# A retention recurrence followed by a Mish feed-forward block: list-scheduled order, early chunks with states carried by TensorE, late DMA transposes

## The chip, the cores and the metric

One core of one Trainium2 chip. The metric is device time in microseconds (us), median of several executions. "Span" is the length of one profiled execution; in the profiled runs of this case the reported time is 1.7 to 1.9 us longer than the span. TensorE is PE in the profile, VectorE DVE, ScalarE ACT, GpSimd POOL, SyncE SP; PEld are TensorE's weight loads.

## The reference

```python
# q, k, v: (B, H, S, D) = (4, 8, 768, 64), float32; w_in: (512, 2048), w_out: (2048, 512)
gamma = 1.0 - 2.0 ** (-5.0 - arange(H))
for t in range(S):                                   # one state of 64x64 per batch and head
    state = gamma * state + outer(k[:, :, t], v[:, :, t])
    y[:, :, t] = q[:, :, t] @ state / sqrt(D)
x = y.transpose(0, 2, 1, 3).reshape(3072, 512)
h = x @ w_in
out = (h * tanh(softplus(h))) @ w_out                # Mish, then the second product
```

## The kernel before

The 3072 tokens are cut into 12 groups of 256 (two chunks of 128; three groups make one batch). In a group, four "units" (pairs of heads) do the recurrence in chunked form. A unit transposes k and q on TensorE, computes the masked products of q and k, updates the state, and forms y from two products that add up in PSUM. Then `f1` is the first product with Mish, in 8 slices per group, and `f2` is the second product.

```python
def step_t(u):                       # transposes on TensorE, three copies on VectorE
    for c in range(CG):
        nc.tensor.transpose(tp[:, 1, c], k16[:, c, hs(hp)], ident)
    for c in range(CG):
        nc.tensor.transpose(tp[:, 0, c], q16[:, c, hs(hp)], ident)
    nc.vector.tensor_copy(kt, tp[:, 1])
    nc.vector.tensor_copy(qp[0:64, :, 0], tp[0:64, 0])      # q padded with zeros, per head
    nc.vector.tensor_copy(qp[64:128, :, 1], tp[64:128, 0])
# step_s: s_ps = kt x qp; am = s_ps * msk; u_ps = k16 x v16; new state = old * gamma**C + u_ps
def step_y(u):
    # ...
        nc.tensor.matmul(y_ps[:, c], v16[:, c, hs(hp)], am[:, c], start=True, stop=st is None)
        if st is not None:                                   # 2 x 128 columns of padded q
            nc.tensor.matmul(y_ps[:, c], st, qp[:, c], start=False, stop=True)
    # ... two half copies to xt on ScalarE

# order of the loads
load(0)
for j in range(NW):
    load_win(j)
load(1); load(2)
# ... cast(0)
for j in range(NW):
    load_wout(j)
load(3)
# order of the work: fixed by hand
for i in range(NG + 2):
    if i + 2 < NG:
        cast(i + 2)                  # q, k, v of two groups ahead, on GpSimd
    if i == 0:
        for j in range(NW):
            cast_wout(j)             # on GpSimd too, behind cast(2)
    # ... load(i + 3)
    for a in range(NSL):             # 8 slices
        # ... the next attention step or steps
        if i < NG:
            f1(i, a)
        if 0 <= i - 2:
            f2(i - 2, a)             # the second product lags by two groups
```

## Time and profile before

| | before |
|---|---|
| median time | 249.91 us (4 runs, 249.44 to 253.05) |
| profiled span | 250.4 us |
| TensorE busy | 220.4 us (88%), 1,696 matmuls |
| TensorE idle before 54 us | 25.2 us |
| last matmul to the end | 3.7 us |

The first view is the second part of the page of the kernel before: busy tenths in 40 equal slices of 6.3 us. PEclk is the clock granted to TensorE.

```profile
PE   0263199949999999999999999999999999999993
...
PEclk9999999998999999999999999999999999999999
DMA  8999999999912914916808609519210111011122
```

TensorE is full from the tenth slice on and mostly empty in the first five. The next view gives busy time in four stretches of the kernel before. Idle time is the length minus the first "busy" figure; the last three columns are granted clock, mean busy share of the DMA engines (as it is counted here it can read above 1), and GB/s.

```profile
core 0: us, PE busy (x) PEld busy (x) DVE busy (x) ACT busy (x) POOL busy (x), PEclk, DMA share, GB/s
0.00:22.00 22.00, 8.04 (x44) 4.85 (x44) 11.29 (x34) 4.94 (x10) 3.54 (x8) 1.00 1.05 285
22.00:54.00 32.00, 20.81 (x189) 17.27 (x189) 19.70 (x46) 13.80 (x29) 25.31 (x12) 1.00 1.16 272
54.00:246.70 192.70, 191.58 (x1463) 135.37 (x1463) 84.88 (x230) 76.53 (x157) 56.25 (x26) 0.99 0.43 97
246.70:250.40 3.70, 0.00 (x0) 0.00 (x0) 0.64 (x1) 0.00 (x0) 0.00 (x0) 0.92 0.19 71
```

From 54 us on there is 1.1 us of idle time in 193, so nearly only less TensorE work can shorten that stretch. (From 55 to 59 us the granted clock is 0.57, which costs 1.7 us more, right after a wait of 3.7 us.) In front of it 14.0 + 11.2 us are idle. What those wait for is in the chain of waits (the work that ended last, followed back), in order of time:

```profile
12.25 11.25 DMA raw_q<-in_q_dram
23.63 2.32 POOL q_276 L119
26.37 1.99 POOL k_277 L121
...
47.47 5.45 DMA raw_k<-in_k_dram
53.08 1.91 POOL k_504 L121
55.48 1.71 PE h_ps L228 x8
```

The q of group 1 (raw_q) sits behind 4 MB of w_in and lands at 23.5 us; its casts on GpSimd follow. The k of group 3 (raw_k, cast as k_504) lands at 52.9 us. In between TensorE has only attention of groups 0 to 2 and first products of groups 0 and 1: the fixed order puts the transposes of group 3's first unit before the last first products of group 1, and has no second product before the first product of group 2. So TensorE waits 3.7 us for k_504, until 55.0 us.

The groups of instructions show the rates:

```profile
L228 PE MATMUL h_ps<-xt,win_87 128*128 128x256 f16 x768 | 101.9, 277 | 0.0
L241 PE MATMUL o_ps<-wout_88,gt 128*128 128x512 f16 x384 | 95.9, 379 | 0.0
L209 PE MATMUL y_ps<-qpad_91,tstate 128*128 128x256 f16 x28 | 7.4, 285 | 0.0
```

After the first bar stand the busy time of the group and the mean duration of one in ns, after the second the idle time before them. Matmuls overlap, so the pace is not that mean: in the timeline eight h_ps start within 0.87 us (109 ns each).

### The profile page before, as it was taken

How to read it: one execution, taken by the hardware profiler on the slowest of the kernel's cores; microseconds unless marked ns; L12 is line 12 of the kernel's file. 1: busy time of each engine (PE TensorE's matmuls, PEld its weight loads, DVE VectorE, ACT ScalarE, POOL GpSimd, SP SyncE). 2: the span in 40 equal slices, each digit the busy share in tenths (PEclk: the TensorE clock that was granted, in tenths of full speed). 3: DMA queues.
4: the chain of work that ended last, by engine and by line, in shares of the span. 5: the costliest groups of instructions: out<-in, count | busy, mean ns of one | idle time of the engine just before them, and what ended most of it. 6: DMA issues, size and time to landing. Idle time of an engine off the chain costs nothing.

```text
span 250.4 us, 4251 instructions
## 1 busy us (share of the span) xinstructions
PE 220.4 (88%) x1696; PEld 157.5 (63%) x1696; DVE 116.5 (47%) x309; ACT 95.3 (38%) x195; POOL 85.1 (34%) x45
## 2 busy tenths in 40 slices
PE   0263199949999999999999999999999999999993
PEld 0141178827777777777777777777777777766441
DVE  1478567624455454535545553444655444101221
ACT  0324037624434445344444434444443444533000
POOL 3102997679940450460640822703600000000000
PEclk9999999998999999999999999999999999999999
DMA  8999999999912914916808609519210111011122
GB/s 162 297 387 263 218 287 387 256 207 227 181 42 66 225 46 106 195 40 149 190 0 176 162 3 229 106 46 228 66 42 0 45 45 41 3 42 45 44 81 84
DMA packets 82868, 33.91 MB, mean 135 GB/s; under 512 B 75552, under 2 KB 75680, under 8 KB 82848
## 3 DMA queue, kind: packets, MB, share of 16 engines
q1 hardware_dynamic: 82560, 33.56, 56.9%
q8 instruction: 13, 0.21, 0.4%
q10 hardware_dynamic: 288, 0.08, 0.1%
q14 instruction: 7, 0.06, 0.1%
HBM read 27.34 MB, written 6.29 MB: 134 GB/s over the span
## 4 chain that ended last, share of the span: by engine, by line
PE 77%; SPq 9%; DMA 7%; POOL 4%; issue 2%; DVE 0%; POOLq 0%
PE o_ps L241 33%; PE h_ps L228 29%; SPq L103 8%; DMA raw_q<-in_q_dram 4%; PE s_ps L174 3%; PE y_ps L205 3%; PE y_ps L209 3%; DMA raw_k<-in_k_dram 2%; PE tp L157 2%; PE tp L159 2%; PE u_ps L182 1%; SPq L130 1%; POOL q_276 L119 1%; POOL k_277 L121 1%; POOL k_504 L121 1%
## 5 line engine op out<-in xcount | busy, mean ns | idle before, releaser
L228 PE MATMUL h_ps<-xt,win_87 128*128 128x256 f16 x768 | 101.9, 277 | 0.0
L241 PE MATMUL o_ps<-wout_88,gt 128*128 128x512 f16 x384 | 95.9, 379 | 0.0
L232 ACT ACTIVATE gt<-h_ps 128x512 f16<-128x512 f32 x96 | 57.3, 597 | 96.0 <-PE h_ps L228 95.7
L228 PEld LDWEIGHTS <-win_87 128*128 128x128 f16 x768 | 72.7, 99 | 9.6
L241 PEld LDWEIGHTS <-gt 128*128 128x128 f16 x384 | 37.6, 98 | 28.2
L212 ACT CAST xt<-y_ps 64x256 f16<-64x256 f32 x96 | 35.1, 365 | 31.1 <-PE y_ps L209 30.5
L176 DVE TENSOR_TENSOR am<-s_ps,msk 128x512 f16<-128x512 f32 x48 | 33.0, 687 | 26.9 <-PE s_ps L174 26.8
L162 DVE COPY kt<-tp 128x256 f16<-128x256 f16 x48 | 14.0, 291 | 52.3 <-PE tp L159 52.3
L246 DVE COPY osb<-o_ps 128x512 f32<-128x512 f32 x24 | 16.6, 691 | 42.6 <-PE o_ps L241 42.6
L191 DVE SCALAR_TENSOR_TENSOR tstate<-tstate,tab,u_ps 128x128 f16<-128x128 f16 x64 | 21.9, 342 | 1.1
L174 PEld LDWEIGHTS <-kt 128*128 128x128 f16 x96 | 9.9, 105 | 8.7
L209 PEld LDWEIGHTS <-tstate 128*128 128x128 f16 x80 | 8.1, 101 | 4.1 <-DVE tstate L189 0.3
L157 PE MATMUL tp<-idtri,k_142 128*128 128x128 f16 x8 | 1.6, 308 | 10.1 <-DVE k_142 L121 9.2
L157 PE MATMUL tp<-idtri,k_277 128*128 128x128 f16 x8 | 1.3, 260 | 8.6 <-POOL k_277 L121 7.8
L142 POOL CAST wout_88<-wst 128x2048 f16<-128x2048 f32 x4 | 7.6, 1893 | 3.4 <-DMA wst<-in_moe_w_out_dram 3.2
L119 POOL TENSOR_TENSOR q_276<-raw_q,tab 128x1024 f16<-128x1024 f32 x1 | 2.8, 2777 | 16.1 <-DMA raw_q<-in_q_dram 16.1
L157 PEld LDWEIGHTS <-k_142 128*128 128x128 f16 x8 | 0.8, 126 | 10.6 <-DVE k_142 L121 9.2
L209 PE MATMUL y_ps<-qpad_91,tstate 128*128 128x256 f16 x28 | 7.4, 285 | 0.0
L209 PE MATMUL y_ps<-qpad_92,tstate 128*128 128x256 f16 x28 | 7.1, 278 | 0.0
L157 PEld LDWEIGHTS <-k_277 128*128 128x128 f16 x8 | 0.7, 110 | 9.5 <-POOL k_277 L121 8.2
L174 PE MATMUL s_ps<-qpad_91,kt 128*128 128x256 f16 x32 | 6.6, 291 | 0.0
L174 PE MATMUL s_ps<-qpad_92,kt 128*128 128x256 f16 x32 | 6.6, 291 | 0.0
(147 smaller groups left out, 226.9 us busy)
## 6 DMA issues: line engine op xcount, KB each, us to landing
raw_q<-in_q_dram SPq DMA_DIRECT2D x24, 256.0 KB, 5.0
raw_k<-in_k_dram SPq DMA_DIRECT2D x24, 256.0 KB, 5.1
raw_v<-in_v_dram SPq DMA_DIRECT2D x24, 256.0 KB, 5.0
out_dram<-osb SPq DMA_DIRECT2D x24, 256.0 KB, 2.0
wst<-in_moe_w_in_dram SPq DMA_DIRECT2D x4, 1024.0 KB, 9.2
wst<-in_moe_w_out_dram SPq DMA_DIRECT2D x4, 1024.0 KB, 10.4
idtri<-rn_identtri ACTq DMA_DIRECT2D x1, 64.0 KB, 3.1
tab<-rn_tab ACTq DMA_DIRECT2D x1, 10.0 KB, 1.9
```

Of the source, the lines that this page charges most:

```text
L103: nc.sync.dma_start(t[:, c], src[b, :, s0:s0 + C].rearrange("h p d -> p h d"))
L157: nc.tensor.transpose(tp[:, 1, c], k16[:, c, hs(hp)], ident)
L162: nc.vector.tensor_copy(kt, tp[:, 1])
L174: nc.tensor.matmul(s_ps[:, c], kt[:, c], qp[:, c], start=True, stop=True)
L176: nc.vector.tensor_tensor(am, s_ps, msk[:, hs(hp)].unsqueeze(1).broadcast_to((P, CG, 2, C)), op=ALU.mult)
L191: nc.vector.scalar_tensor_tensor(tn, states[-1], tab[:, 2 * H + hp:2 * H + hp + 1], u_ps[:, c], op0=ALU.mult, op1=ALU.add)
L209: nc.tensor.matmul(y_ps[:, c], st, qp[:, c], start=False, stop=True)
L212: nc.scalar.copy(xt[o:o + 64, hp, g * GT:(g + 1) * GT].rearrange("p (c i) -> p c i", i=C), y_ps[o:o + 64, :, hh])
L228: nc.tensor.matmul(h_ps[:, j], win16[:, bp, fb * P:(fb + 1) * P], xt[:, bp, i * GT:(i + 1) * GT], start=(bp == 0), stop=(bp == NBP - 1))
L232: nc.scalar.activation(gts[i][:, 2 * a:2 * a + 2], h_ps, AF.Mish, scale=inv_boost3)
L241: nc.tensor.matmul(o_ps, gts[i][:, fb, t * P:(t + 1) * P], wout16[:, fb], start=(fb == 0), stop=(fb == NFB - 1))
L246: nc.vector.tensor_copy(osb, o_ps)
```

## The change

The intent: keep TensorE fed from about 20 us on, and give it less to do.

1. **Order by a list scheduler.** The kernel describes 916 timed tasks with priorities, dependencies and buffer slots. `Plan.run` simulates five engines, each of which starts the ready task of highest priority, and the instructions are emitted in the simulated order. Attention goes before first products, these before second products; the lag of two groups is gone.
2. **Early groups (0 and 1).** Group 0 is loaded, cast and computed in single chunks, loads are ordered groups 0, 1, w_in, w_out, then 2, 3, 4, and the old state enters the new one through an identity matmul.
3. **Late groups (5 to 11).** k and q are transposed by DMA. In groups 2 to 11 the state is kept block-diagonal, so its product streams 128 columns of unpadded q.
4. y fills full 128 partitions with zero-padded v, so ScalarE evacuates it in one copy.

```diff
+class Plan:
+    LAT = {"PE": 0.25, "DVE": 0.1, "ACT": 0.1, "POOL": 0.12, "DMA": 2.0}
+    # ... tasks, ready heaps by (prio, id), slots counted per buffer tag
+    plan = Plan(
+        {"raw_q": 3, "raw_k": 3, "raw_v": 3, "grp": 3, "wst": 4, "am": 2, "xt": 3,
+         "gt": 5, "out": 2, "tp": 1, "s": 1, "u": 1, "y": 1, "h": 2, "o0": 1, "o1": 1})
+    sts = [[cpool.tile([P, P], FP16, name=f"st{h}_{i}") for i in range(3)] for h in range(HP)]
     # ...
+    def dma_transpose(g):                      # g >= DT = 5
+            nc.sync.dma_start_transpose(
+                casts[g]["kt"].rearrange("p c x j -> p (c x) j"),
+                casts[g]["k16"].rearrange("p c h d -> p (c h d)"))
     # ... the same for q, then VectorE pads q
-            nc.tensor.matmul(y_ps[:, c], v16[:, c, hs(hp)], am[:, c], ...)
-            if st is not None:
-                nc.tensor.matmul(y_ps[:, c], st, qp[:, c], start=False, stop=True)
+                for hh in range(2):
+                    nc.tensor.matmul(
+                        y[:, i], G["vp"][:, c * HP + hp, hh:hh + 2], loc["am"][:, i, hh], ...)
+                if early:
+                    for hh in range(2):
+                        nc.tensor.matmul(y[:, i], st, G["qp"][:, c, hp, hh], ...)
+                else:
+                    nc.tensor.matmul(y[:, i], st, G["qt"][:, c, hp], start=False, stop=True)
     # ...
+    order_dma = [0, 1, ("in", 0), ("in", 1), ("in", 2), ("in", 3),
+                 ("out", 0), ("out", 1), ("out", 2), ("out", 3), 2, 3, 4]
     # ...
+    order, end = plan.run()
+    for start, seq, fn, e, d in order:
+        fn(e)
```

## The prediction

> **What bounds the kernel now.** TensorE. By stretches of the profile: from 54.0 to 246.7 us it is busy 191.6 of 192.7 us; before 54 us only 28.9 us, so 25 us of TensorE time are lost at the start; the last 3.7 us are the final copy (0.69) and store. The chain of waits says what bounds the start: input DMA, loads and casts (raw_q landing, POOL q/k casts) until about 53 us; afterwards only o_ps and h_ps matmuls (62%) and attention matmuls.
>
> Streamed columns counted from the code: 393,216 in the two feed-forward products, 104,448 in attention, in 1,696 matmuls. The Trainium skill ("TensorE: Matmul & The Clock Gate", Back-to-back issue gap) gives N/2.4 + 2.5 ns for one matmul; this trace agrees (8 h_ps of 256 columns start-to-start 0.87 us, 4 o_ps of 512 in 0.865, attention pairs of 128 in 0.11). Sum: 207.4 + 4.2 = 211.6 us.
>
> **What the change does.**
> 1. TensorE work. DMA transposes for groups 5-11 remove 14,336 columns. Block-diagonal state lets the state product of groups 2-11 stream 128 instead of 256 columns: 68 x 128 = 8,704 fewer. Carrying state by an identity matmul adds 1,536. The attention-times-v product keeps its columns, in twice as many matmuls. New total 476,160 columns, about 1,704 matmuls: 202.7 us (estimate by the same formula), 8.9 less, all on the critical path.
> 2. Start. Group 0 goes in single chunks; groups 0 and 1 load first, then w_in, w_out, then groups 2-4. From the trace, 256 KB of q/k/v cost 1.15-1.18 us of queue time and 1 MB of weights about 2.7 us (387 GB/s slices). So group 1 lands at about 17, w_in at 20-28, w_out at 31-39, group 2 at 46 us. Dense feed-forward work should start at about 21 us instead of 54 (28 us for groups 0 and 1 cover the wait for w_out and group 2). I expect a gap of 1-4 us at about 52-58 us, because group 2's four attention units are VectorE-bound (about 2.9 us each: copies 1.15, mask 0.69, state 1.1).
> 3. The list schedule places attention matmuls with no slack on modelled times; the old order had a whole f1+f2 slice (1.74 us) between dependent steps. I charge 4 us of small TensorE stalls, and 1.7 us for a cold clock when the dense part starts.
> 4. DMA transposes: 14 of 256 KB. The Trainium skill ("Advanced Engine Details and Errata", X-Bar Transpose) calls them as fast as regular DMAs; no trace here shows it. Queues are 40-60% busy after 60 us, so I expect them hidden.
> 5. ScalarE evacuates y in 48 full-width copies instead of 96 half ones (365 ns each); VectorE gains state half-copies and the q padding. Both stay under 75% busy: no direct effect.
>
> **Sum.** Dense start 21 + remaining work (202.7 - about 6 of attention done earlier) 197 + cold clock 1.7 + gap 2.5 + stalls 4 = 226; tail 3.7 gives 230; measured times are slightly below the profiled span: 229 us.
>
> Predicted 229 us, range 221 to 241. Chances: faster by over 2% 0.93, within 2% 0.05, slower 0.02.
>
> **What would show it.** TensorE dense from about 21 us; TensorE busy about 208-212 us; no tp matmuls for groups 5-11; y_ps state products at 128 columns; idle before attention matmuls ended by VectorE or ScalarE, 3-8 us in total; same tail; TensorE share about 91%.
>
> **What would make it wrong.** DMA transposes taking several times 2.3 us and blocking the SyncE queue ahead of loads and stores; zero-slack order stalling TensorE in every unit (over 10 us); weight loads binding the 128-column y matmuls; group 2 arriving later than 50 us. If stalls are nil, about 222.

## The result and the profile after

| | before | after |
|---|---|---|
| median time | 249.91 us | 230.99 us (4 runs, 229.37 to 232.23) |
| ratio | | 0.9215, 95% interval 0.912 to 0.931 |
| profiled span | 250.4 us | 227.6 us |
| TensorE busy | 220.4 us | 210.3 us, 1,704 matmuls |
| TensorE idle in the span | 30.0 us | 17.3 us |

A ratio here is the mean time of one kernel's fast runs over that of the kernel before in the same rounds, so it is not quite the ratio of the two medians. The span fell by 22.8 us: 10.1 less busy and 12.7 less idle. The time fell by 19 us in the medians, because the profiled run of the kernel before took 252.17 us, 2.3 us above its median, and that of the changed kernel was the fastest of its four.

Busy tenths of the changed kernel:

```profile
PE   0588999997899999999999999999999999999993
...
PEclk9999999999999999999999999999999999999999
DMA  7999999997999988998989909111012010122212
```

The stretches of the changed kernel, the columns as before:

```profile
core 0: us, PE busy (x) PEld busy (x) DVE busy (x) ACT busy (x) POOL busy (x), PEclk, DMA share, GB/s
0.00:22.00 22.00, 11.70 (x96) 8.15 (x97) 17.25 (x49) 13.27 (x39) 10.66 (x19) 1.00 1.00 264
22.00:54.00 32.00, 32.00 (x262) 22.79 (x261) 16.11 (x38) 16.96 (x28) 7.25 (x5) 1.00 0.99 306
54.00:224.10 170.10, 166.58 (x1351) 118.78 (x1348) 90.77 (x234) 60.02 (x119) 37.29 (x24) 1.00 0.54 128
224.10:227.60 3.50, 0.00 (x0) 0.00 (x0) 0.65 (x1) 0.00 (x0) 0.00 (x0) 0.96 0.19 75
```

From 22 to 54 us TensorE is now never idle (11.2 us before). Idle time after 54 us has grown from 1.1 to 3.5 us. In the chain of waits the start now reads:

```profile
20.79 0.96 ACT win_90 L196
21.79 1.05 PE h_ps L643 x8
...
32.19 0.86 PE o_ps L665 x4
...
56.09 4.69 DMA raw_k<-in_k_dram
60.87 1.23 DVE k_555 L346
62.12 0.70 DVE am L513
62.87 0.38 PE y_ps L600 x4
```

The first product begins at 21.8 us, right after the first cast of w_in, and the second product (o_ps) already at 32.2 us. The rates are those of before, and the state product (st) is at 128 columns. In the groups, the product of v with the masked scores (am) is now twice as many matmuls of half the width:

```profile
L643 PE MATMUL h_ps<-xt,win_90 128*128 128x256 f16 x768 | 94.8, 273 | 0.3
L665 PE MATMUL o_ps<-wout_91,gt 128*128 128x512 f16 x384 | 89.8, 379 | 0.0
L600 PE MATMUL y_ps<-am,vpad_95 128*128 128x128 f16 x64 | 7.5, 233 | 1.4 <-DVE am L513 1.0
L610 PE MATMUL y_ps<-qt,st_0_98 128*128 128x128 f16 x6 | 1.3, 219 | 0.0
```

In the timeline four of the products with am take 0.22 us until the next matmul starts (62.87 to 63.09 us), 55 ns each, so the weight loads do not bind them.

The new gap, in the timeline of the changed kernel (start, duration, engine, line; the bracket is the idle time just before and what ended it):

```profile
54.48 0.69 DVE L676 COPY osb<-o_ps 128x512 f32<-128x512 f32 x1
...
55.21 0.69 DVE L513 TENSOR_TENSOR am<-s_ps,msk 128x512 f16<-128x512 f32 x1
...
55.95 0.28 PE L600 MATMUL y_ps<-am,vpad_97 128*128 128x128 f16 x2 [1.23 <-DVE am L513]
...
56.85 0.39 PE L504 MATMUL s_ps<-qpad_94,kt 128*128 128x256 f16 x2 [0.39 <-DVE qpad_94 L491]
...
58.17 0.28 PE L600 MATMUL y_ps<-am,vpad_97 128*128 128x128 f16 x2 [0.36 <-DVE am L513]
```

From 51.5 to 60.1 us VectorE is busy for 8.2 of 8.6 us, on the units of group 2 and the first of group 3, and between them on output copies (osb) of group 1, while TensorE has run out of older work. One more piece of the gap is not of this kind. In the chain above, VectorE stands still for 0.73 us before 60.87 until the k of group 4 (k_555) lands, the mask product am comes behind it in program order, and TensorE waits 0.64 us, until 62.87.

The DMA transposes, in the list of DMA issues of the changed kernel (last figure: us from issue to landing):

```profile
raw_q<-in_q_dram SPq DMA_DIRECT2D x24, 256.0 KB, 3.7
...
out_dram<-osb SPq DMA_DIRECT2D x24, 256.0 KB, 2.0
...
qt<-q_893 SPq DMA_TRANSPOSE x1, 4.1
kt<-k_894 SPq DMA_TRANSPOSE x1, 2.9
```

All 14 land in 2.7 to 4.3 us. From 80 to 130 us the DMA engines are 0.93 busy, against 0.57 before. I had forecast 0.4 to 0.6.

### The profile page after: what moved, and what is told of

Its sections match the earlier page's. It is cut to its first block, busy times and chain, and to the rows that moved or that the text cites. A ratio compares the mean times of both kernels' runs of the same rounds, so it can differ in the third digit from the quotient of the medians.

```text
span 227.6 us, 4297 instructions
## 1 busy us (share of the span) xinstructions
PE 210.3 (92%) x1704; PEld 149.7 (66%) x1704; DVE 124.8 (55%) x319; ACT 90.2 (40%) x185; POOL 55.2 (24%) x47
## 4 chain that ended last, share of the span: by engine, by line
PE 83%; DVE 9%; DMA 3%; ACT 2%; issue 1%; SPq 0%; ACTq 0%; DVEq 0%
PE h_ps L643 35%; PE o_ps L665 34%; PE y_ps L600 5%; PE s_ps L504 4%; DMA raw_k<-in_k_dram 2%; DVE am L513 2%; DVE msk L277 2%; PE y_ps L610 1%; DVE qpad_93 L427 1%; PE u_ps L565 1%; DMA idtri<-rn_identtri 1%; DVE osb L676 1%; DVE k_116 L346 1%; DVE k_555 L346 1%; ACT qpad_93 L196 0%
## 5 line engine op out<-in xcount | busy, mean ns | idle before, releaser
L643 PE MATMUL h_ps<-xt,win_90 128*128 128x256 f16 x768 | 94.8, 273 | 0.3
L665 PE MATMUL o_ps<-wout_91,gt 128*128 128x512 f16 x384 | 89.8, 379 | 0.0
L643 PEld LDWEIGHTS <-win_90 128*128 128x128 f16 x768 | 73.8, 98 | 12.7 <-ACT win_90 L196 0.4
L648 ACT ACTIVATE gt<-h_ps 128x512 f16<-128x512 f32 x96 | 57.2, 597 | 60.4 <-PE h_ps L643 60.1
L513 DVE TENSOR_TENSOR am<-s_ps,msk 128x512 f16<-128x512 f32 x40 | 27.6, 691 | 8.8 <-PE s_ps L504 7.7
L196 ACT CAST xt<-y_ps 128x256 f16<-128x256 f32 (+1 forms) x52 | 18.4, 354 | 34.7 <-PE y_ps L610 32.6
L600 PE MATMUL y_ps<-am,vpad_95 128*128 128x128 f16 x64 | 7.5, 233 | 1.4 <-DVE am L513 1.0
L600 PE MATMUL y_ps<-am,vpad_97 128*128 128x128 f16 x64 | 7.1, 219 | 1.8 <-DVE am L513 1.6
L600 PEld LDWEIGHTS <-vpad_97 128*128 128x128 f16 x64 | 5.4, 98 | 4.2 <-DVE am L513 2.1
L462 PE MATMUL tq<-idtri,q_115 128*128 128x128 f16 x8 | 2.5, 310 | 5.9 <-POOL q_115 L341 5.9
L600 PEld LDWEIGHTS <-vpad_95 128*128 128x128 f16 x64 | 5.1, 101 | 4.3 <-DVE am L513 1.8
L504 PE MATMUL s_ps<-qpad_92,kt 128*128 128x256 f16 x32 | 7.6, 300 | 0.2 <-DVE kt L198 0.2
L600 PE MATMUL y_ps<-am,vpad_96 128*128 128x128 f16 x64 | 7.3, 219 | 0.3 <-ACT xt L196 0.3
L513 DVE TENSOR_TENSOR am<-s_ps,idtri 128x256 f16<-128x256 f32 (+1 forms) x12 | 6.1, 511 | 1.7 <-PE s_ps L504 1.5
L600 PEld LDWEIGHTS <-vpad_96 128*128 128x128 f16 x64 | 5.6, 98 | 1.4 <-issue 0.5
L504 PE MATMUL s_ps<-qpad_93,kt 128*128 128x256 f16 x32 | 6.1, 272 | 0.4 <-DVE am L513 0.4
L504 PE MATMUL s_ps<-qpad_94,kt 128*128 128x256 f16 x32 | 6.1, 273 | 0.4 <-DVE qpad_94 L491 0.4
L198 DVE CAST wout_91<-wst 128x1024 f16<-128x1024 f32 x4 | 2.8, 694 | 6.3 <-DMA wst<-in_moe_w_out_dram 6.3
```

The lines of the kernel that those rows point to most:

```text
L196: nc.scalar.copy(dst, src)
L198: ENG[e].tensor_copy(dst, src)
L462: nc.tensor.transpose(loc["tq"][:, i], G["q16"][:, c, hs(hp)], ident)
L504: nc.tensor.matmul(t[:, i], G["kt"][:, c, hp], G["qp"][:, c, hp], start=True, stop=True)
L513: nc.vector.tensor_tensor(am, loc["s"], m, op=ALU.mult)
L600: nc.tensor.matmul(y[:, i], G["vp"][:, c * HP + hp, hh:hh + 2], loc["am"][:, i, hh], start=(hh == 0), stop=(st is None and hh == 1))
```

## The experiments

Theory: the gain is (a) second products that fill the wait for w_out and group 2, (b) TensorE time saved by the DMA transposes, one for one, and (c) the narrower state product; what is left is the gap at 50 to 65 us, a VectorE queue. Rivals are named with each run. Runs came in three sets, each set on one chip beside its own runs of the kernel before; the first and third sets include the changed kernel itself as a yardstick.

| run | median us | ratio to before | state of the result |
|---|---|---|---|
| set 1: e0_after | 229.70 | 0.9109 (0.904 to 0.918) | correct |
| e1_pe_transposes | 235.58 | 0.9342 (0.927 to 0.941) | correct |
| e2_wide_state | 231.61 | 0.9201 (0.913 to 0.928) | correct |
| e3_f2_lag | 238.90 | 0.9464 (0.938 to 0.955) | correct |
| set 2: e4_before_loads | 257.12 | 1.0184 (1.011 to 1.026) | correct |
| e5_act_copy | 226.92 | 0.9007 (0.891 to 0.911) | correct |
| e6_dmat_from3 | 233.17 | 0.9193 (0.908 to 0.930) | wrong, error 0.286 |
| e7_whole_g0 | 228.88 | 0.9073 (0.901 to 0.914) | correct |
| set 3: e11_after_again | 231.11 | 0.9167 (0.912 to 0.922) | correct |
| e9_act_whole | 225.92 | 0.8989 (0.893 to 0.905) | correct |
| e10_three_undone | 247.80 | 0.9843 (0.978 to 0.991) | correct |
| e8_dmat3_guarded | 230.13 | 0.9135 (0.908 to 0.919) | correct |

### The yardstick: e0_after

No edit.

> The changed kernel again, as the yardstick for the runs beside it. Expected about 231 us (ratio to before 0.92), TensorE idle of about 3.6 us after 21 us, most of it between 50 and 63 us. Every difference below is against this run of the same rounds.

Measured 229.70 us. TensorE idles 1.9 us from 50 to 65 us instead of 2.8. But here the granted clock fell to half, from about 57.7 to 61.1 us, which it did not in the profile shown above:

```profile
58.00:60.50 2.50, 2.24 (x15) 1.61 (x15) 2.36 (x9) 0.37 (x1) 1.90 (x1) 0.50 1.11 259
```

Busy time times missing clock, summed in steps of 0.5 us, gives 1.6 us lost. Part of the "busy" time of this run is therefore slow time, and the same program may or may not pay it.

### Transposes back on TensorE: e1_pe_transposes

```diff
     DT = 5
+    TT = 12
-        if g >= DT:
+        if g >= TT:              # both places; casts stay as they were
             dma_transpose(g)
```

> Undo one part: groups 5 to 11 are transposed on TensorE again (their casts stay on GpSimd). My theory: the DMA transposes are hidden and give exactly their TensorE time, so 112 matmuls of 128 columns come back, 6.2 us, about 237 us. Rival: the transposes fill the DMA queues (busy share about 0.9 from 60 to 130 us where I forecast 0.4 to 0.6) and delay loads, so that they return less than they save: then this run is less than 3 us slower than the changed kernel, or faster. In the trace the DMA share from 80 to 130 us should fall from about 0.9 to about 0.5 either way.

Measured +5.9 us over the yardstick (235.58 against 229.70; by the ratios +2.6%, also 5.9). TensorE busy rises by 6.0 us to 217.3. From 80 to 130 us the DMA share falls from 0.98 in the yardstick to 0.68, not to 0.5. The theory holds: the transposes give back nothing, although the queues are nearly full. They have time to spare: in the profile of the changed kernel those of group 5 are issued at 66.9 and 69.2 us and land 4.1 and 2.9 us later, and group 5's first score product (s_ps) starts at 80.5 us.

### Full-width state product: e2_wide_state

```diff
-                if early:
+                if True:
                     for hh in range(2):
                         nc.tensor.matmul(y[:, i], st, G["qp"][:, c, hp, hh], ...)
```

(and the time of this step in the plan)

> Undo one part: the state product of groups 2 to 11 streams both padded halves of q, 2 x 128 columns, as the early groups do, instead of the unpadded 128. My theory: 68 more matmuls of 128 columns on a saturated TensorE, 3.8 us, about 235 us. Rival: at 128 columns per weight load the weight load and not the stream sets the pace, so that the narrow product saved less than the column count says: then the difference is under 2 us.

Measured +1.9 us by the medians and +1.0% (2.3 us) by the ratios; the profiled spans differ by 4.1 us. This is between theory and rival, so the time alone does not decide. The pace is plain in the timeline of this run, where the two state matmuls of a chunk take 0.11 us until the next matmul starts:

```profile
76.45 0.28 PE L607 MATMUL y_ps<-qpad,st 128*128 128x128 f16 x2
76.56 0.38 PE L504 MATMUL s_ps<-qpad,kt 128*128 128x256 f16 x2
```

The single one of the changed kernel takes about 0.055 us (80.41 to 80.47 us, for example). So each narrow product saves its full 55 ns, 3.8 us for 68 of them, and the weight load does not bind. TensorE busy agrees: 213.38 us against 211.35, which holds 1.6 us of slow clock (this run has 1.00 from 50 to 65 us), so 2.0 + 1.6 = 3.6. The profiled run here is the slowest of its four (233.39 us, the others 231.46 to 231.76) and has 1.4 us of idle time from 80 to 130 us where the yardstick has 0.2. Why the medians differ by less than 3.6 stays open.

### The lag of the second products: e3_f2_lag

```diff
-                       dp + ([prev] if prev else [pre_o]),
+                       dp + ([prev] if prev else
+                             [pre_o] + ([f1t[i + 2, 0]] if i + 2 < NG else [])),
```

(and the second products are described after all first products, in a loop of their own)

> Undo one part of the order: loads, engines and operations as in the changed kernel, but the second product of group i may not start before the first product of group i+2 has begun, which is the lag that the kernel before had by hand. My theory: the 14 us of second products of groups 0 and 1 are what TensorE does while the weights w_out and group 2 arrive; without them TensorE idles between about 36 and 58 us, and the run is 11 to 14 us slower, about 243 us, nearly all of the gain at the start. Rival (the gain at the start comes from the order of loads, not from the order of work): under 4 us slower.

Measured +9.2 us. The mechanism is the one expected, the split is not. In the stretches of this run, TensorE idles from 36 us on and then runs at half clock:

```profile
40.00:44.00 4.00, 1.03 (x8) 0.68 (x7) 1.66 (x2) 1.54 (x3) 0.00 (x0) 1.00 0.95 216
44.00:48.00 4.00, 1.83 (x15) 1.47 (x16) 2.81 (x8) 0.00 (x0) 1.04 (x1) 0.67 1.03 233
48.00:52.00 4.00, 3.08 (x23) 2.07 (x22) 3.78 (x14) 0.74 (x2) 3.49 (x2) 0.50 1.07 243
52.00:56.00 4.00, 3.53 (x28) 2.55 (x27) 3.71 (x14) 0.39 (x2) 2.74 (x3) 0.50 1.01 228
```

Against the yardstick's profile the span is 10.8 us longer: 5.1 us more idle (21.14 against 16.05) and 5.7 us more busy time with the same matmuls (217.06 against 211.35). The slow clock, counted as for the yardstick, takes 5.6 us here and 1.6 there, so 4.0 of the 5.7; the rest is not explained. The Trainium skill ("TensorE: Matmul & The Clock Gate", Why this matters for your kernels) warns of idle gaps over about 3 us between matmul bursts; the 3.3 us wait at 41.5 us here agrees. I had expected all of the loss as idle time.

### The order of loads alone: e4_before_loads

The kernel before, with

```diff
 load(0)
+load(1)
 for j in range(NW):
     load_win(j)
-load(1); load(2)
 # ...
 for j in range(NW):
     load_wout(j)
+load(2)
 load(3)
```

> One part alone: the kernel before, with only the order of its loads changed to that of the changed kernel (groups 0 and 1, then the first weights, then the second weights, then groups 2 and 3). My theory: the fixed order of work still puts the attention of group 2 and both first products ahead of any second product, so TensorE starves until group 2 has landed at about 46 us anyway; within 3 us of before, 247 to 253 us. Rival: the order of loads alone gives the gain at the start: 8 us or more faster than before, under 242 us.

Measured 1.8% slower than before, 257.12 us. The rival falls: the order of loads alone gives no gain. It is also slower than my range. TensorE has two long waits. The first, 8.2 us until 30.2 us, is ended by VectorE, whose fixed order puts the casts of w_in before the copies of group 1's first unit. The second, 7.6 us until 47.2 us, is ended by GpSimd's cast of group 2's k, and the GpSimd timeline of this run shows why:

```profile
17.53 2.77 POOL L125 TENSOR_SCALAR v<-raw_v 128x1024 f16<-128x1024 f32 x1 [0.41 <-DMA raw_v<-in_v_dram]
42.94 1.90 POOL L119 TENSOR_TENSOR q<-raw_q,tab 128x1024 f16<-128x1024 f32 x1 [22.63 <-DMA raw_q<-in_q_dram]
...
50.41 7.41 POOL L142 CAST wout<-wst 128x2048 f16<-128x2048 f32 x4
57.79 1.90 POOL L119 TENSOR_TENSOR q<-raw_q,tab 128x1024 f16<-128x1024 f32 x1
```

GpSimd takes its work in program order. It waits 22.6 us for group 2, and the casts of w_out and of group 3 stand behind that. An order of loads and an order of work have to be changed together.

### Relieving VectorE in the gap: e5_act_copy

```diff
-            e1 = add({"DVE": 1.15}, ekq, pr, ...)
+            e1 = add({"DVE": 0.87}, ekq, pr, ...)                  # without the copy of qt
+            e2 = add({"ACT": act(256)} if g == 2 else {"DVE": 0.28}, eqt, pr, [t1], ...)
-        e1 = add({"DVE": 0.7}, ev, (13, i, t), ...)
+        e1 = add({"ACT": 0.65} if i < 2 else {"DVE": 0.7}, ev, (13, i, t), ...)
```

> Take one suspected wait away: in the changed kernel TensorE idles about 2.8 us between 50 and 63 us, where VectorE is 0.9 busy with the four units of group 2 and with the output copies of groups 0 and 1, while ScalarE is under 0.2 busy. Here ScalarE makes those four output copies and one of the four transposed copies of group 2. My theory: the gap is a VectorE queue, so TensorE idle from 50 to 63 us falls to under 1.3 us and the time falls by 1 to 2.5 us, to about 229 us. Rival: the gap is the late landing of group 2 and 3 from DMA: idle stays above 2.3 us and the time stays.

Measured 226.92 us; TensorE idle from 50 to 65 us is 1.44 us:

```profile
50.00:65.00 15.00, 13.56 (x133) 10.17 (x131) 12.91 (x45) 6.14 (x14) 9.67 (x6) 1.00 1.03 244
```

There is no yardstick in this set, and the intervals of the ratios overlap those of the changed kernel (0.9109, 0.9167, 0.9215), so the step is likely but not settled by this run alone. The idle time has halved against 2.8 and fallen by a quarter against the 1.9 of the yardstick; it missed the expected 1.3 by a little. The cast of group 4's k, too, has moved from VectorE to GpSimd in the new plan, so the wait for its landing (0.64 us above) is gone as a side effect. It speaks for the VectorE queue; e9_act_whole below comes back to it.

### DMA transposes from group 3: e6_dmat_from3

```diff
     DT = 5
+    TT = 3                      # transposes by DMA from group 3; casts as before
```

> More of one part: DMA transposes from group 3 on instead of group 5. If they are hidden there too, 32 matmuls leave TensorE (1.8 us) and VectorE loses about 5 us of copies between 57 and 90 us: about 229 us. Rival: the queues are full there (busy share 1.1 from 60 to 80 us) and the transposes delay groups 3 to 5: TensorE idles between 60 and 100 us by 2 us or more beyond the 0.8 of the changed kernel, and the run is the same or slower.

The result was wrong, relative error 0.286, so its time (233.17 us) proves nothing by itself. Following the emitted order and noting which group last wrote each state buffer shows 8 state products that read a buffer already overwritten by a later group (chunk 1 of group 3 and chunk 0 of group 4, all four pairs of heads). The plan counts slots for 16 buffer kinds, but the ring of three state buffers is not among them. With transposes that arrive late for group 3, the plan runs state updates of group 4 before the y of group 3, and of group 5 before the y of group 4. The synchronization then faithfully keeps that wrong order. In the changed kernel itself the same count is 0: it is right by its timing constants, not by construction.

### The same, guarded: e8_dmat3_guarded

```diff
                            [u1] + ([bdep] if bdep is not None else []) +
+                           [y for _, _, tn in chain for y in readers.pop(id(tn), [])],
     # ... after each y task:
+        for c, st in ins:
+            if st is not None:
+                readers.setdefault(id(st), []).append(y1)
```

> e6_dmat_from3 gave a wrong result. Its emitted order has 8 state products that read one of the three state buffers after a later group has overwritten it: the plan knows slots for the other buffers but none for these. Here the state update of a buffer also waits in the plan for the products that read it. My theory of the wrong result: this run is correct. Rival (the DMA transposes themselves go wrong when four are queued together): it stays wrong with an error near 0.29. Time: as e6_dmat_from3 or up to 2 us slower, 231 to 235 us, so that transposing groups 3 and 4 by DMA is no gain over the changed kernel; if the overwritten buffers were what slowed e6_dmat_from3, about 228.

Correct, and 230.13 us against 231.11 for the yardstick of its set (ratios 0.9135 and 0.9167, intervals overlapping): no gain that can be told from zero. So the missing guard was the cause of the wrong result, and the transposes were not. 32 matmuls less (1.8 us) are paid back by TensorE idle time: 1.8 us from 65 to 100 us, where the yardstick has 0.2. Its four waits (0.68, 0.45, 0.44 and 0.22 us) are ended by VectorE, not by a DMA. Five was a good place to begin.

### Group 0 whole: e7_whole_g0

```diff
-        cast(g, bufs[g], [[0], [1]] if g == 0 else [[0, 1]])
+        cast(g, bufs[g], [[0, 1]])
-        for cs in ([[0], [1]] if g == 0 else [[0, 1]]):
+        for cs in [[0, 1]]:
```

(and its loads in the order of the other groups)

> Undo one part: group 0 is loaded, cast and computed whole (256 tokens at a time) instead of in two chunks of 128. The dense part of TensorE starts at 21.8 us in the changed kernel, when group 0's attention and the first cast of the first weights end together. My theory: it now starts 1 to 3 us later, but what group 2 needs from DMA and VectorE (until about 58 us) is unchanged, and the 2.8 us gap before that absorbs most of the delay: under 1.2 us slower than the changed kernel. Rival: every us lost at the start is a us of the total: 2 us or more slower.

Measured 228.88 us, not slower than the changed kernel in any set. TensorE idle before 22 us rises from 10.3 to 12.5 us, and idle from 50 to 65 us is 1.1 us instead of 1.9 to 3.2. The profile also runs at half clock as the dense part starts (0.60 from 22 to 26 us, 1.7 us lost), which that of the changed kernel does not. The later start is absorbed, as expected: what group 2 needs from DMA and VectorE sets the date, not the start. The short chunks of group 0, a named part of the change, earn nothing.

### Three parts undone: e10_three_undone

The edits of e1, e2 and e3 together.

> Three parts undone at once: late transposes on TensorE, full-width state product, and the lag of two groups for the second products. Singly they cost 5.9, 2.3 and 9.2 us. If they are the change, and independent, this run stands 17 us above the changed kernel, 245 to 249 us, within 2 per cent of the kernel before, and what is left (list order, loads, engines) is worth under 5 us. If one of them hides another (TensorE work coming back into the idle time that the lag opens), it is 10 to 13 us, about 241.

Measured 247.80 us, 16.7 us above the yardstick of its set, where the single costs 5.9 + 2.3 + 9.2 sum to 17.4. The three parts are independent within the noise and make up nearly all of the gain. What is left between this run and the kernel before is a ratio of 0.984, about 4 us: list order, load order, engines and early chunks together.

### A faster version: e9_act_whole and its yardstick e11_after_again

The edits of e5 and e7 together, beside the unedited changed kernel.

> The changed kernel once more, as the yardstick for the three runs beside it: about 230 us, ratio to before about 0.915.

> A version to beat both: ScalarE makes the output copies of groups 0 and 1 and one copy of group 2 (as in e5_act_copy), and group 0 is computed whole (as in e7_whole_g0). The two touch the same gap, so their gains should not add fully: TensorE idle from 50 to 65 us under 1 us, idle before 22 us about 12.5, and about 226.5 us, 1 to 2 per cent below the changed kernel. If the two gains were independent it would be 225 or less; if the later start is no longer absorbed once the gap is filled, it is 228, between the two.

Measured 225.92 us against 231.11 us on the same chip, ratios 0.8989 (0.893 to 0.905) and 0.9167 (0.912 to 0.922): 1.9% faster than the changed kernel, 10% faster than the kernel before. The row of the gap, first the yardstick, then this version:

```profile
50.00:65.00 15.00, 11.82 (x108) 8.16 (x107) 12.90 (x39) 3.61 (x8) 6.91 (x5) 1.00 0.93 224
```

```profile
50.00:65.00 15.00, 15.00 (x146) 11.40 (x145) 12.89 (x43) 6.37 (x15) 8.45 (x6) 1.00 0.99 242
```

TensorE's idle time there goes from 3.2 us to zero, with ScalarE busy 6.4 us instead of 3.6. The order of loads is the same but for group 0's, so the gap was not mainly the landing of group 2. But this run changes two things, and each alone already shrinks the gap: to 1.4 us with the copies on ScalarE (e5), to 1.1 us with group 0 whole (e7), which leaves TensorE more work for later. So VectorE's queue is shown as the last link of the three waits of the gap that every profile of the changed kernel has (about 1.2, 0.4 and 0.3 us); how much of the closing is due to which edit is not separated, and the yardstick's 3.2 us contain 0.99 us behind the late k of group 4, which is cast on GpSimd in this run as in e5. Up to 150 us the idle sum is 12.0 against 14.6 us. The other part of the spans' difference of 3.9 us is TensorE busy time, 208.7 against 209.9; the profiles give no single cause for that.

## Why the prediction was right

The mechanism and the size held: 229 us predicted, 230.99 measured. Term by term:

| step of the prediction | predicted | the profile after |
|---|---|---|
| dense start | 21 us | first h_ps at 21.8 us, no idle from 22 to 50 us |
| work remaining then | 197 us | 198.8 us busy from 21.8 to 224.1 us |
| cold clock | 1.7 us | 0 in this profile; 1.6 us in e0_after, but at 57.7 to 61.1 us; 1.7 us at the dense start in e7_whole_g0 |
| gap at group 2 | 2.5 us | 2.8 us (50 to 65 us) |
| small stalls from zero slack | 4 us | 0.6 us (65 to 150 us) |
| tail | 3.7 us | 3.5 us |
| span | 230 us | 227.6 us |
| time minus span | -1 us | +1.8 us |

- Two errors cancelled. The term "I charge 4 us of small TensorE stalls" was mis-sized: 0.6 us; the 1.7 us for a cold clock, which the profile of the kernel before has after its wait of 3.7 us, did not come in this profile. That the order without slack hardly stalls may be due to the timing constants, most of which are close to the chip (0.875 us for a slice of the first product against 0.87 in the trace, 1.15 for the copies of a unit against 1.13), though not all (0.35 us for one mask table against a mean of 0.75 and a median of 0.43); no run tested this. And "measured times are slightly below the profiled span" came from comparing the span of one run with the median of others; the profiled run of the kernel before took 252.17 us for its span of 250.4.
- TensorE work: the columns counted from the code gave 8.9 us less; busy time fell by 10.1, of which 1.7 is the slow clock that the kernel before paid from 55 to 59 us, so the work itself fell by about 8.4. The DMA transposes gave 5.9 us (6.2 counted). The state product gave 55 ns per matmul in the pace but 2.3 us in the time (3.8 counted).
- "Hidden" DMA transposes: right (e1). The reason I gave, queues 40 to 60% busy, was wrong: 0.93 from 80 to 130 us. They are hidden because they are done early (group 5's some 8 us before its first score product). From group 3 on they earn nothing (e8).
- The gap: its place, its size and its cause (group 2's units bound by VectorE) were forecast. Less VectorE work together with a later start closes it (e9); e5 and e7 alone leave 1.4 and 1.1 us of it, and up to 1 us of it was a wait for group 4's k that nobody forecast.
- The start: the second products of groups 0 and 1 "cover the wait". e3 shows 9.2 us for that alone. That the order of loads is not enough by itself was shown by e4.
- Not foreseen: the chunking of group 0 is worth nothing (e7), and the slow clock added 4.0 us to 5.1 us of idle time (e3).

## What to carry to other kernels

Where a saturated engine is idle only at the start, ask what work it could do with the data already landed, and free that work from a fixed lag; reordering the loads without reordering the work can cost time. Before tuning an early stage, look for the next wait behind it: a later start cost nothing measurable here (e7), because later waits absorbed it. A scheduler that emits program order protects only the buffers that it is told of; every ring of buffers has to be a slot or a dependency, and a test that passes shows only that the present timing is harmless.

## What the Trainium skill lacked or had wrong

- "Advanced Engine Details and Errata", X-Bar Transpose (TRN2), says that transpose DMAs are as fast as regular DMAs and expects 350 to 400 GB/s. Here 14 SBUF-to-SBUF transposes of 256 KB landed in 2.7 to 4.3 us, like the loads of 256 KB (3.7 to 4.3 us) and slower than the stores of the same size (2.0 us). By the time of the queue's packets (64.3% of 227.4 us in e0_after, 52.6% of 233.5 us in e1_pe_transposes) one costs about 1.7 us of all queues, an estimate from these two profiles, so about 157 GB/s, under half of the page's figure. By the same kind of count the loads of q, k and v cost 1.6 us each (share 1.35 at 218 GB/s from 23 to 30 us in the kernel before), so "as fast as regular DMAs" is not contradicted. No run measured one alone.
- "TensorE: Matmul & The Clock Gate", Why this matters for your kernels, speaks of idle gaps over about 3 us; as a rule for when the clock stays up this sentence was not enough here. In e0_after the clock was at half from about 57.7 to 61.1 us although no idle piece there was longer than 1.23 us (1.9 us in all); in another run of the same program, with 2.8 us of idle time, it stayed at 1.00. The 3.3 us wait of e3_f2_lag was followed by half clock from 48 to 56 us.
- The page's figure for one matmul, N/2.4 + 2.5 ns (Back-to-back issue gap), agreed at 128, 256 and 512 columns (55, 109 and 216 ns start to start in these traces), also where each matmul of 128 columns has its own weight load. The same section also gives sustained paces with weight loads of about 81 ns at 128 columns and 131 ns at 512; these traces show 55 and 216.
